# Attention values fetched in token order by five transfers a batch, and seven stage tiles instead of three for the first batch's weights

## The chip, the cores and the metric

The kernel runs on one core of a Trainium2 chip. The metric is the device time of one execution in microseconds (us), lower is better; three executions of the kernel before are at hand, and one further execution was profiled.

## The reference

Three blocks follow one another. Nystrom attention with 32 landmarks over 4 batches of 8 heads, 576 tokens and 64 values a head; then a gated MLP on the 2304 tokens of all batches; then a second MLP.

```python
q_lm = q.reshape(B, H, m, S // m, D).mean(axis=3)      # m = 32, S // m = 18
k_lm = k.reshape(B, H, m, S // m, D).mean(axis=3)
A = sm(q, k_lm); Bm = sm(q_lm, k_lm); C = sm(q_lm, k)  # softmax(scale * a @ b.T)
Z = Bm.T / (norm1(Bm) * norminf(Bm) + 1e-06)
for _ in range(6):
    Z = 2 * Z - Z @ Bm @ Z
x = A @ Z @ C @ v                                      # then to (2304, 512)
xn = x / sqrt(mean(x * x) + 1e-06) * rms_g
x = (silu(xn @ w_gate) * (xn @ w_val)) @ w_out         # d_ff = 1536
out = (s * relu(x @ w_in) ** 2 + b) @ w_out2           # d_ff = 2048
```

The sum over tokens in C @ v may run in any order, if C's columns and v's rows stand in the same one. The weights arrive as 64-bit floats.

## The kernel before

**Order of work.** No engine chooses its work on the chip. While the program is built, a planner (`Scheduler.run`) keeps a list of operations with planned costs, a due key and the buffers that each needs, and writes them one by one into the five engines' queues: the lowest key among those that can start. The queues then run in that order, and an instruction that has to wait holds all that stand behind it in its queue. SyncE (SP) issues nearly all transfers; a transfer's planned cost is split into its landing (all of it) and the hold on SP (the cost less 2.0 us). At most eight transfers are on their way at a time: a ninth is issued when one of the eight has landed.

**Attention.** `attention(b, ...)` is written once for each batch. Batch 0 runs alone at the start; batches 1 to 3 fill gaps of the gated MLP of the batch before. A batch loads k and q by four or more transfers (L458, L463) and v by eighteen (L476): v's tile has tokens on its partitions, and each transfer fills 32 partitions with the 32 tokens of one residue `i * 18 + n`, all heads, as pieces of 256 bytes. C's scores are made in two halves of 288 columns, in that same order of residues; the exponential (L701, ScalarE) writes them side by side into the tile eC, five transposes on TensorE (L718) bring tokens to the partitions, and L740 multiplies with v. v of a later batch goes into the same tile, so its transfers wait for L740 of the batch before.

**The gated MLP.** `units` are pairs of a batch and one of 12 slices f of 128 hidden columns. A unit needs the slice of w_gate and of w_val in single precision, side by side in one of three `rawg` tiles. For batch 0 they come from the 64-bit inputs by `narrow`: a load of 512 KB into a stage tile (L934), three operations of ScalarE on it (L951, L953, L961; the last may go to VectorE as L962), and one of VectorE (L965) that writes the half of rawg. The stage tile is free again after L961. When both halves stand, rawg is stored to DRAM (L978), from where batches 1 to 3 read it (L981); a rawg tile is taken again after its store has landed and after L1034 has read it. L1034 folds the attention's last matrix into the slice (uh, ul through L1044, L1045, L1047), L1059 is the slice's matmuls, L1075, L1077 and L1081 the gating. From unit 6 on, the output matmuls (L1104, L1108) and the narrowing of w_out (L932, tile rawo, store L990, later reads L992) come in between. The second MLP (L1016, L1134) ends the program.

**Stage tiles.** There are three for all uses (`st_r`). The gate and value slices of batch 0 take from a longer ring, in which three more tiles lie in the second half of the buffer xbuf and stay closed until the attention of batch 0 is done:

```python
st_late = [Slot(far[:, :, 256 * i:256 * i + 256].bitcast(I64)) for i in range(3)]
st0_r = Ring(st_r.slots + st_late)
```

The first half of xbuf is written for the first time when the gated MLP's result of batch 0 is evicted (L1118). Up to the planned time 60 the planner also fills gaps of TensorE with matmuls whose result nobody reads (L1291).

Of the kernel before, what the change touches and what calls it, by code (L numbers as in the profile page):

```python
# [37 lines left out]
XC = 2.0  # L38
COLD1 = 6.5
GV = 8  # L40
W2_STEP = 4.2


# [207 lines left out]
def tile_nystrom_attention_two_mlps(  # L251
# [117 lines left out]
    st_late = [Slot(far[:, :, 256 * i:256 * i + 256].bitcast(I64)) for i in range(3)]  # L369
    for x in st_late:  # L370
        x.held = True
    st0_r = Ring(st_r.slots + st_late)

    def xb(c, c0, n):
        return [("x", c, i) for i in range(c0 // 32, (c0 + n) // 32)]
# [34 lines left out]
    def attention(b, t0, t1):  # L410
# [60 lines left out]
            return vs.t.rearrange("p (j h d) -> p j h d", j=5, h=H)  # L471

        def load_v(e):
            sv = v[b].rearrange("h (i n) d -> n i h d", n=SEG)
            for n in range(SEG):
                e.dma_start(out=vt()[32 * (n % 4):32 * (n % 4) + 32, n // 4], in_=sv[token(b, n)])  # L476

        at(("sp", 9.5), -0.25 if b else 0.01, load_v, w=[vs])


        def loaded(g, h):
# [200 lines left out]
        def c_side(g, p0):  # L682
            for j in (g,) if fine else (0, 1) if g == 0 else ():
                transposed("k", j, p0)
            pC = [Buf(ps_r), Buf(ps_r)]
            eC = Buf(eC0_r if first else eC_r)
            cm, cs, rc = Buf(sm_r), Buf(sm_r), Buf(sm_r)
            for hf in range(2):
                scores(pC[hf], "k", g, hf, p0, [(pC[1], "taken")] if hf else [],
                       [(pC[1], "taken"), (eC, "taken")] if hf == 0 else [])  # L690
                at(("dve", t_dve(HC)), p0 + 0.02, lambda e, hf=hf: e.tensor_reduce(
                    out=cm.t[:, hf:hf + 1], in_=pC[hf].t[:, 0:HC], axis=AX, op=ALU.max),
                    r=[pC[hf]], w=[(cm, hf)])

            def c_max(e):
                e.tensor_reduce(out=cm.t[:, 2:3], in_=cm.t[:, 0:2], axis=AX, op=ALU.max)
                e.tensor_scalar(out=cm.t[:, 3:4], in0=cm.t[:, 2:3], scalar1=-scale, scalar2=None, op0=ALU.mult)

            at(("dve", 0.32), p0 + 0.02, c_max, r=[(cm, 0), (cm, 1)], w=[(cm, 3)])
            for hf in range(2):  # L700
                at(("act", t_act(HC) + 0.19), p0 + 0.03, lambda e, hf=hf: e.activation(  # L701
                    out=eC.t[:, HC * hf:HC * hf + HC], in_=pC[hf].t[:, 0:HC], func=ACTF.Exp,
                    scale=scale, bias=cm.t[:, 3:4], accum_out=cs.t[:, hf:hf + 1]),
                    r=[pC[hf], (cm, 3)], w=[(eC, hf), (cs, hf)])

            def c_rec(e):
                e.tensor_tensor(out=rc.t[:, 0:1], in0=cs.t[:, 0:1], in1=cs.t[:, 1:2], op=ALU.add)
                e.tensor_scalar(out=rc.t[:, 0:1], in0=rc.t[:, 0:1], scalar1=1e-9, scalar2=None, op0=ALU.add)
                e.reciprocal(out=rc.t[:, 0:1], in_=rc.t[:, 0:1])

            at(("dve", 0.5), p0 + 0.05, c_rec, r=[(cs, 0), (cs, 1)], w=[rc])
            pE = [Buf(ps_r), Buf(ps_r)]
            eT = Buf(eT_r)

            def tr(_, js):
                for j in js:
                    n = min(128, S - 128 * j)
                    nc.tensor.transpose(  # L718
                        pE[j // 4].t[0:n, 128 * (j % 4):128 * (j % 4) + 128],
                        eC.t[:, 128 * j:128 * j + n], ident)  # L720

            at(("pe", slow * 0.5), p0 + 0.04, lambda e: tr(e, range(4)), r=[(eC, 0), (eC, 1), "ident"],
               w=[pE[0], (pE[1], "taken"), (eT, "taken")])
            at(("pe", 0.13), p0 + 0.04, lambda e: tr(e, [4]), r=[(eC, 1), "ident", (pE[1], "taken")], w=[pE[1]])

            def ev(e, o, i):
                if e is nc.scalar:
                    e.activation(out=o, in_=i, func=ACTF.Copy)
                else:
                    e.tensor_copy(out=o, in_=i)  # L730

            at({"act": t_act(512), "dve": t_dve(512)}, p0 + 0.05, lambda e: ev(e, eT.t[:, 0:512], pE[0].t), r=[pE[0]], w=[(eT, 0)])
            at({"act": t_act(128), "dve": t_dve(128)}, p0 + 0.05, lambda e: ev(e, eT.t[0:64, 512:640], pE[1].t[0:64, 0:128]), r=[pE[1]], w=[(eT, 1)])
            pV = Buf(ps_r)

            def cv_mm(_):
                for j in range(5):
                    n = min(128, S - 128 * j)
                    for h in range(4):
                        nc.tensor.matmul(  # L740
                            out=pV.t[32 * h:32 * h + 32, 0:D],
                            lhsT=eT.t[0:n, 128 * j + 32 * h:128 * j + 32 * h + 32],
                            rhs=vt()[0:n, j, 2 * h + g, :], start=(j == 0), stop=(j == 4))

            at(("pe", 1.3), p0 + 0.06, cv_mm, r=[(eT, 0), (eT, 1), vs], w=[pV, (Cv, "taken")])
            at({"dve": t_dve(64), "act": 0.1 + t_act(64)}, p0 + 0.07, lambda e: (
                e.activation(out=Cv.t[:, D * g:D * g + D], in_=pV.t[:, 0:D], func=ACTF.Copy, scale=rc.t[:, 0:1])
                if e is nc.scalar else e.tensor_scalar(
                    out=Cv.t[:, D * g:D * g + D], in0=pV.t[:, 0:D], scalar1=rc.t[:, 0:1], scalar2=None, op0=ALU.mult)),
                r=[pV, rc], w=[(Cv, g)])  # L750
# [167 lines left out]
    def narrow(key, kind, f, part, dst, w, after=()):  # L918
        c = slice(128 * f, 128 * f + 128)
        wt = ((w_gate, w_val, w_out), (w_in2, None, w_out2))[kind - 1][part]  # L920
        rows = kind == 1 and part < 2
        st, a, m = Buf(st0_r if rows else st_r), Buf(ca_r), Buf(cm_r)

        def wide(x):
            return x.rearrange("p (k f) -> p k f", k=KD) if rows else x

        def staged():
            return wide(st.t) if len(st.t.shape) == 2 else st.t

        def load(e):  # L930
            if part == 2:
                e.dma_start(out=staged(), in_=wt[c, :])  # L932
            else:
                e.dma_start(out=staged() if rows else st.t.rearrange("p (k f) -> p k f", k=KD),  # L934
                            in_=wt[:, c].rearrange("(k p) f -> p k f", p=128))

        def word(i):
            x = staged().bitcast(I32)
            if rows:
                return x.rearrange("p k (n t) -> p k n t", t=2)[:, :, :, i]  # L940
            return x.rearrange("p (n t) -> p n t", t=2)[:, :, i]

        n_ops = len(S_.ops)
        op(("sp", 3.46), key - 12, load, w=[st])
        def low():
            x = staged().bitcast(U8)
            if rows:
                return x.rearrange("p k (n t) -> p k n t", t=8)[:, :, :, 3]
            return x.rearrange("p (n t) -> p n t", t=8)[:, :, 3]

        op(("act", 0.08 + t_act(512)), key, lambda e: e.activation(  # L951
            out=wide(a.t), in_=word(1).bitcast(F32), func=ACTF.Copy, scale=2.0 ** -112), r=[st, "stage"], w=[a])
        op(("act", 0.08 + t_act(512)), key, lambda e: e.activation(  # L953
            out=wide(m.t), in_=low(), func=ACTF.Copy, scale=1.0 / 32, bias=-31.0 / 64), r=[st, "stage"], w=[m])

        def upper():
            return wide(m.t).bitcast(F16).rearrange("p k (n t) -> p k n t", t=2)[:, :, :, 1] if rows else (
                m.t.bitcast(F16).rearrange("p (n t) -> p n t", t=2)[:, :, 1])

        op({"act": 0.08 + t_act(512), "dve": t_dve(512)}, key, lambda e: (  # L960
            e.activation(out=upper(), in_=word(1).bitcast(F32), func=ACTF.Copy, scale=2.0 ** -100)  # L961
            if e is nc.scalar else e.scalar_tensor_tensor(  # L962
                out=wide(m.t), in0=word(1), scalar=-2 ** 31, in1=wide(m.t),
                op0=ALU.bitwise_and, op1=ALU.bitwise_or)), r=[st, m, "stage"], w=[m], pair=True)
        op(("dve", t_dve(512)), key, lambda e: e.scalar_tensor_tensor(  # L965
            out=dst().bitcast(I32), in0=a.t.bitcast(I32), scalar=3, in1=m.t,
            op0=ALU.logical_shift_left, op1=ALU.bitwise_or), r=[a, m, *after], w=[w], pair=True)
        for o in S_.ops[n_ops + 1:]:
            o.after = RELC

# [117 lines left out]
    def out_mm(key, b, hf, f):  # L1088
# [27 lines left out]
        for c in range(KD):  # L1116
            op({"act": t_act(HC), "dve": t_dve(HC)}, key, lambda e, c=c: (
                e.activation(out=xbuf[:, c, c0:c0 + HC], in_=A[c].t[:, 0:HC], func=ACTF.Copy) if e is nc.scalar  # L1118
                else e.tensor_copy(out=xbuf[:, c, c0:c0 + HC], in_=A[c].t[:, 0:HC])),
                r=[A[c], "far"], w=xb(c, c0, HC))  # L1120

    acc = {}

# [103 lines left out]
    for n in range(len(units) + HALF + 1):  # L1227
        t = T[n]
        if n < len(units):
            b, f = units[n]  # L1230
            if f == 0:
                if b + 1 < B:
                    attention(b + 1, *at_time(b + 1))
# [94 lines left out]
```

## Time and profile before

| what | value |
|---|---|
| median of three executions | 877.86 us (877.86 to 879.12) |
| profiled execution, time | 878.94 us |
| profiled execution, span of its instructions | 876.9 us |
| TensorE busy | 850.0 us (97%) |
| VectorE busy | 684.2 us (78%) |
| ScalarE busy | 471.5 us (54%) |
| GpSimd busy | 109.9 us (13%) |
| share of the chain that ended last: TensorE, VectorE, ScalarE, DMA | 82%, 8%, 4%, 2% |
| transferred | 105.96 MB, 121 GB/s over the span |

Busy time is that of instructions of the engine itself; SP only issues and is not counted as busy. The chain that ended last is followed back from the last instruction, at each step to what released it. A busy share over the whole span is a mean over stages with different limits, so the sections below go by stretches of it.

### The profile page before, as it was taken

Reading aid. Unit: us, or ns where it says so; the run is one execution under the profiler, and the core shown is the slowest. Engines: PE = TensorE matmul, PEld = TensorE weight load, DVE = VectorE, ACT = ScalarE, POOL = GpSimd, SP = SyncE. Lnnn points to the kernel's source line nnn. Section 1 sums busy time; section 2 is a strip of 40 time slices with the busy share of each in tenths; the row PEclk is TensorE's granted clock in tenths of the full one; section 3 lists DMA queues with packets and bytes.
Section 4 is the critical chain, followed back from the end, with each engine's and each line's share of the span. In section 5 each row is a group of like instructions: output and inputs, shape, how many; then the busy total and the mean of one; then the engine's idle time right before and its main releaser. Section 6 shows DMA issues by size and latency. Waiting matters only on the chain.

```text
span 876.9 us, 16944 instructions
## 1 busy us (share of the span) xinstructions
PE 850.0 (97%) x6397; PEld 714.7 (82%) x6397; DVE 684.2 (78%) x1494; ACT 471.5 (54%) x968; POOL 109.9 (13%) x148
## 2 busy tenths in 40 slices
PE   8969999999999999999999999999999999999997
PEld 5647767888889888899999888888888888888896
DVE  6868788888998888899999866766676667666786
ACT  4869877346554455478988433433343334333454
POOL 0260046212750123200000000000000000000000
PEclk8989999999999999999999999999999999999999
DMA  7797996876534332369976000010001000100100
GB/s 219 222 350 257 297 272 208 245 232 204 145 112 154 121 99 97 135 202 297 311 229 197 1 1 0 12 37 1 1 15 34 1 1 19 29 1 1 34 16 24
DMA packets 72513, 105.96 MB, mean 121 GB/s; under 512 B 25584, under 2 KB 46064, under 8 KB 72432
## 3 DMA queue, kind: packets, MB, share of 16 engines
q1 hardware_dynamic: 72240, 104.62, 38.4%
q8 instruction: 50, 0.82, 0.4%
q14 instruction: 31, 0.25, 0.1%
q10 hardware_dynamic: 192, 0.26, 0.1%
HBM read 90.70 MB, written 14.16 MB: 120 GB/s over the span
## 4 chain that ended last, share of the span: by engine, by line
PE 82%; DVE 8%; ACT 4%; DMA 2%; issue 2%; SPq 1%; DVEq 0%; ACTq 0%
PE bank L1016 23%; PE bank L1134 22%; PE bank L1059 14%; PE bank L1108 14%; PE bank L1034 3%; PE bank L844 1%; PE bank L1104 1%; PE bank L598 1%; SPq L476 1%; PE bank L660 1%; DMA region<-in_k_dram 1%; PE bank L1291 1%; DVE wl L914 1%; DMA xbuf<-in_moe_w_val_dram 1%; ACT cmag L953 1%
## 5 line engine op out<-in xcount | busy, mean ns | idle before, releaser
L1059 PE MATMUL bank<-xh,uh 128*128 128x288 f32 x384 | 123.1, 320 | 5.6 <-DVE hbuf L1077 4.7
L1269 ACT ACTIVATE hbuf<-bank 128x512 f32<-128x512 f32 (+1 forms) x79 | 43.9, 556 | 144.2 <-PE bank L1016 143.3
L1016 PE MATMUL bank<-xh,uh 128*128 128x512 f32 (+1 forms) x320 | 117.7, 368 | 1.0 <-ACT hbuf L1269 1.0
L1016 PE MATMUL bank<-xh,ul 128*128 128x512 f32 (+1 forms) x320 | 117.7, 368 | 0.0
L1016 PE MATMUL bank<-xl,uh 128*128 128x512 f32 (+1 forms) x320 | 117.6, 368 | 0.0
L1059 PE MATMUL bank<-xl,uh 128*128 128x288 f32 x384 | 113.6, 296 | 0.0
L1059 PE MATMUL bank<-xh,ul 128*128 128x288 f32 x384 | 113.6, 296 | 0.0
L1134 PE MATMUL bank<-wh,hh 128*128 128x512 f32 x288 | 112.4, 390 | 0.3 <-DVE hh L913 0.3
L1134 PE MATMUL bank<-wl,hh 128*128 128x512 f32 x288 | 112.3, 390 | 0.0
L1134 PE MATMUL bank<-wh,hl 128*128 128x512 f32 x288 | 112.0, 389 | 0.0
L1108 PE MATMUL bank<-hh,wh 128*128 128x288 f32 x336 | 101.3, 302 | 0.1
L1108 PE MATMUL bank<-hl,wh 128*128 128x288 f32 x336 | 99.0, 295 | 0.0
L1108 PE MATMUL bank<-hh,wl 128*128 128x288 f32 x336 | 98.8, 294 | 0.2 <-DVE wl L914 0.2
L1059 PEld LDWEIGHTS bank<-xh,uh 128*128 128x128 f32 x384 | 72.7, 189 | 24.9 <-DVE hbuf L1077 6.8
L914 DVE TENSOR_TENSOR hl<-hbuf,hh 128x512 fp32r<-128x512 f32 (+2 forms) x135 | 77.9, 578 | 2.6
L1059 PEld LDWEIGHTS bank<-xl,uh 128*128 128x128 f32 x384 | 72.8, 189 | 0.5
L1059 PEld LDWEIGHTS bank<-xh,ul 128*128 128x128 f32 x384 | 72.6, 189 | 0.0
L1016 PEld LDWEIGHTS bank<-xh,uh 128*128 128x128 f32 x320 | 60.1, 188 | 12.4 <-ACT hbuf L1269 1.2
L1016 PEld LDWEIGHTS bank<-xl,uh 128*128 128x128 f32 x320 | 60.0, 188 | 11.1
L1016 PEld LDWEIGHTS bank<-xh,ul 128*128 128x128 f32 x320 | 60.1, 188 | 10.1
L1108 PEld LDWEIGHTS bank<-hh,wh 128*128 128x128 f32 x336 | 63.0, 188 | 4.4 <-issue 2.3
L913 DVE CAST uh<-region 128x512 fp32r<-128x512 f32 x56 | 23.9, 426 | 54.4 <-PE bank L1016 54.4
(207 smaller groups left out, 1787.6 us busy)
## 6 DMA issues: line engine op xcount, KB each, us to landing
rawo<-kepto SPq DMA_DIRECT2D x84, 256.0 KB, 3.2
rawg<-keptg SPq DMA_DIRECT2D x36, 512.0 KB, 3.9
stage<-in_moe_w_out_dram SPq DMA_DIRECT2D x28, 512.0 KB, 4.6
stage<-in_moe_w_in_dram SPq DMA_DIRECT2D x16, 512.0 KB, 5.0
keptg<-rawg SPq DMA_DIRECT2D x12, 512.0 KB, 6.6
region<-in_v_dram SPq DMA_DIRECT2D x72, 64.0 KB, 2.5
stage<-in_moe_w_val_dram SPq DMA_DIRECT2D x8, 512.0 KB, 6.7
xbuf<-in_moe_w_gate_dram SPq DMA_DIRECT2D x7, 512.0 KB, 7.0
```

The lines of the kernel that those rows point to most:

```text
L476: e.dma_start(out=vt()[32 * (n % 4):32 * (n % 4) + 32, n // 4], in_=sv[token(b, n)])
L598: nc.tensor.matmul(out=ps.t[p, pn * g:pn * g + n], lhsT=lhsT(p, g), rhs=rhs(p, g), start=True, stop=True)
L660: nc.tensor.matmul(out=ps.t[:, 0:HC], lhsT=part(u, "bd")[:, 128 * e:128 * e + 128], rhs=part(y, "t").rearrange("p (t e i) -> p t e i", e=2 ...
L844: nc.tensor.matmul(out=pX2[i].t[:, 0:HC], lhsT=WBD.t[p, 128 * g:128 * g + 128], rhs=AT[hf, g].t[p, 0:HC], start=True, stop=True)
L913: else e.tensor_copy(out=hi(), in_=src())), r=r, w=[wh], pair=True)
L914: b = op({"dve": t_dve(n), "pool": t_pool(n)}, key, lambda e: e.tensor_tensor(out=lo(), in0=src(), in1=hi().bitcast(F32), op=ALU.subtract) ...
L1016: nc.tensor.matmul(out=ps.t[:, 0:n], lhsT=w[a].t[:, ks], rhs=x[y].t[:, kd, 0:n], start=(kd == 0 and i == 0), stop=(kd == KD - 1 and i == 2))
L1034: nc.tensor.matmul(out=pU[g].t[m, 0:256], lhsT=gw[b].t[p, m], rhs=r.t[p, :, 128 * k:128 * k + 128], start=True, stop=True)
L1059: nc.tensor.matmul(out=ps.t[:, 0:HC], lhsT=u[a].t[:, 256 * g + 128 * part:256 * g + 128 * part + 128], rhs=x[y].t.rearrange("p k n -> p (k ...
L1108: nc.tensor.matmul(out=A[c].t[:, 0:HC], lhsT=w[a].t[:, 128 * c:128 * c + 128], rhs=hs[y].t[:, 0:HC], start=(f == 0 and i == 0), stop=(f == ...
L1134: nc.tensor.matmul(out=A[c].t, lhsT=hs[a].t[:, s], rhs=w[y].t, start=(f == 0 and i == 0), stop=(f == F2 - 1 and i == 2))
L1269: e.activation(out=r.t[:, 0:n], in_=ps.t[:, 0:n], func=ACTF.Relu) if e is nc.scalar
```

## The change

v is loaded by five transfers a batch, each of 128 tokens (the last of 64) in the order of the sequence, onto 128 partitions; the pieces of 256 bytes stay. The exponentials of C are written to eC at the columns of their tokens: neighbours in the instruction's order then lie 18 elements apart. The planned cost of v's load falls from 9.5 to 5.0. Four stage tiles in the first half of xbuf are added for batch 0's gate and value slices, open from the start. A gate in the planner's list, at the first unit of batch 1, keeps evictions that are listed after it behind all operations on these tiles.

```diff
+V_SP = 5.0
-    st0_r = Ring(st_r.slots + st_late)
+    st_near = [Slot(xbuf[:, :, 256 * i:256 * i + 256].bitcast(I64)) for i in range(4)]
+    st0_r = Ring(st_r.slots + st_near + st_late)
+    row_ops = []
         def load_v(e):
-            sv = v[b].rearrange("h (i n) d -> n i h d", n=SEG)
-            for n in range(SEG):
-                e.dma_start(out=vt()[32 * (n % 4):32 * (n % 4) + 32, n // 4], in_=sv[token(b, n)])
-        at(("sp", 9.5), -0.25 if b else 0.01, load_v, w=[vs])
+            for j in range(5):
+                n = min(128, S - 128 * j)
+                e.dma_start(out=vt()[0:n, j], in_=v[b][:, 128 * j:128 * j + n].rearrange("h n d -> n h d"))
+        at(("sp", V_SP), -0.25 if b else 0.01, load_v, w=[vs])
+            def in_order(hf):
+                x = eC.t[:, 0:S]
+                if fine:
+                    return x.rearrange("p (i n) -> p n i", i=M)[:, HB * hf:HB * hf + HB]
+                return x.rearrange("p (i t e) -> p e t i", i=M, e=2)[:, hf]
-                    out=eC.t[:, HC * hf:HC * hf + HC], in_=pC[hf].t[:, 0:HC], func=ACTF.Exp,
+                    out=in_order(hf), in_=pC[hf].t[:, 0:HC].rearrange("p (t i) -> p t i", i=M), func=ACTF.Exp,
+        if rows:
+            row_ops.extend(S_.ops[n_ops:])
-                r=[A[c], "far"], w=xb(c, c0, HC))
+                r=[A[c], "far", "near"], w=xb(c, c0, HC))
+            if n == F1:
+                gate("near", row_ops, t)
```

## Rows read from the trace of the kernel before

**Rows 1.** Busy time of each engine by stretch, granted clock, DMA share.

```profile
10.00:20.00 10.00, 7.79 (x123) 4.15 (x122) 7.96 (x33) 4.15 (x13) 0.67 (x1) 0.84 0.60 150
...
42.26:80.00 37.74, 28.99 (x262) 23.23 (x261) 27.69 (x62) 28.35 (x60) 14.76 (x21) 0.91 0.89 300
...
80.00:130.00 50.00, 48.34 (x577) 33.98 (x575) 40.13 (x110) 41.78 (x94) 10.50 (x14) 1.00 0.93 281
130.00:240.00 110.00, 106.90 (x1041) 90.75 (x1041) 96.80 (x224) 60.33 (x136) 44.72 (x57) 1.00 0.69 212
```

**Rows 2.** Timeline of SP's issues, 0 to 60 us: start, duration, line, transfer, count.

```profile
2.67 13.33 SPq L476 DMA_DIRECT2D region<-in_v_dram  x18
16.05 0.45 SPq L934 DMA_DIRECT2D stage<-in_moe_w_gate_dram  x1
...
18.23 0.79 SPq L395 DMA_DIRECT2D gT<-in_moe_rms_g_dram  x1
...
28.92 14.54 SPq L476 DMA_DIRECT2D region<-in_v_dram  x18
43.55 0.40 SPq L934 DMA_DIRECT2D stage<-in_moe_w_val_dram  x1
...
47.09 1.66 SPq L978 DMA_DIRECT2D keptg<-rawg  x1
```

**Rows 3.** The chain that ended last, 36 to 82 us: start, duration, what.

```profile
43.55 4.91 DMA stage<-in_moe_w_val_dram
...
57.01 2.88 PE bank L1059 x12
...
61.38 1.78 PE bank L1059 x12
```

**Rows 4.** Timeline of ScalarE, with the idle time before and what ended it.

```profile
17.44 0.50 ACT L701 ACTIVATE region<-bank,region 128x288 f32<-128x288 f32 x1 [1.46 <-DVE region L697]
...
20.50 0.66 ACT L951 ACTIVATE ca<-stage 128x512 f32<-128x512 f32 x1 [1.98 <-DMA stage<-in_moe_w_gate_dram]
...
48.48 0.67 ACT L951 ACTIVATE ca<-stage 128x512 f32<-128x512 f32 x1 [3.14 <-DMA stage<-in_moe_w_val_dram]
```

**Rows 5.** Timeline of TensorE.

```profile
25.03 1.31 PE L740 MATMUL bank<-region 128*32 128x64 f32 x40
...
42.26 0.51 PE L1059 MATMUL bank<-xh,uh 128*128 128x288 f32 x1
...
53.18 1.22 PE L1034 MATMUL bank<-rawg,gw 64*32 64x256 f32 x16 [3.31 <-DVE hbuf L1077]
```

**Rows 6.** Matmuls of L1291 alone, by stretch: busy time of TensorE first.

```profile
42.26:80.00 37.74, 2.73 (x11) 1.41 (x11) 0.91 0.89 300
```

**Rows 7.** Transfers from 11 to 16 us, when only v's eighteen moved: packets, share of 16 engines.

```profile
DMA packets 2241, 0.56 MB, mean 111 GB/s; under 512 B 2240, under 2 KB 2240, under 8 KB 2240
...
q1 hardware_dynamic: 2240, 0.54, 48.4%
```

**Rows 8.** Groups of ScalarE's instructions, 42.26 to 80 us: count, busy us, mean ns.

```profile
L961 ACT ACTIVATE cmag<-stage 128x512 f16<-128x512 f32 x7 | 5.5, 782 | 0.1
```

**Rows 9.** Groups of VectorE's instructions, 42.26 to 80 us.

```profile
L965 DVE SCALAR_TENSOR_TENSOR rawg<-ca,cmag 128x512 int32<-128x512 int32 x11 | 9.3, 849 | 3.3 <-ACT cmag L961 3.3
```

**Rows 10.** Stores of line L978, 43.5 to 70 us: from issue to landing.

```profile
DMA to landing us min/median/max: 5.3/8.7/9.5
```

**Rows 11.** Timeline of VectorE.

```profile
56.04 1.89 DVE L965 SCALAR_TENSOR_TENSOR rawg<-ca,cmag 128x512 int32<-128x512 int32 x2
```

**Rows 12.** The chain that ended last, 146 to 164 us.

```profile
146.96 0.42 SPq L476
...
156.11 0.45 SPq L476
...
156.67 3.17 DMA rawo<-kepto
```

**Rows 13.** Timeline of TensorE, 144 to 166 us: the rows with idle time before them.

```profile
156.81 0.40 PE L1059 MATMUL bank<-xh,uh 128*128 128x288 f32 x1 [1.31 <-DVE hbuf L1077]
```

## The prediction

> **What bounds the kernel now.** I read the page's 40 slices first, then busy time by stretch, then the chain that ended last, then the queue of SP, then single engines where the chain pointed. The page says TensorE, 97% of the span; by stretch that is true from 80 us on, and untrue before. From 42.26 us, where the first matmul of the gated MLP starts [rows 5], to 80 us TensorE is busy for 28.99 of 37.74 us, while the DMA engines are at 0.89 [rows 1]. Of the busy time 2.73 us are filling matmuls [rows 6], and twelve matmuls of L1059 took 2.88 us at 57 us where twelve took 1.78 us at 61 us [rows 3]; the granted clock, 0.91 over the stretch [rows 1], had fallen to the lower of its two levels after the long gap. So some 8.75 + 2.73 + 1.1 = 12.6 us of this stretch are no work. After it TensorE idles 1.66 of 50 us and 3.1 of 110 us.
>
> Why it idles is read from the chain: at 43.55 us a load of a value slice is issued and waited for during 4.91 us [rows 3]. ScalarE stands 3.14 us for it [rows 4], and TensorE 3.31 us before L1034 of the third slice [rows 5]. The load was not late because the memory was slow: SP issued v of batch 1 from 28.92 to 43.46 us, eighteen transfers, and the load stood behind them [rows 2]. Batch 0's v had held SP from 2.67 to 16.00 us in the same way. While only v moved, the DMA engines were 48% busy [rows 7]: idle bandwidth, then a queue at full share.
>
> **The change part by part.**
>
> *v's issue.* Before, 18 instructions hold SP for 13.33 us and 14.54 us (batches 0 and 1) [rows 2], and for some 9.6 us in batch 2, 146.96 to 156.56 us [rows 12]. After, 5. What is unknown is the price of an issue with 1024 pieces. Lower end: an issue of a stage load, 512 pieces, takes 0.45 us [rows 2], as one of v's 256 pieces does in row 156.11 [rows 12]; with some 0.04 us between issues five take 2.5 us. Upper end: gT's issue, 512 pieces of 4 bytes, took 0.79 us [rows 2]; if the price grew with the pieces, 0.45 us for 256 would be 1.8 us for 1024, and five would hold SP for 9 us, little less than now. I take the lower end, since the larger stage load pays no more, but not less than the moving itself where free places among the eight run out: 2240 pieces in 5 us at 48.4% of 16 engines are 17.3 ns each [rows 7], so the 576 x 8 = 4608 pieces of a batch need 5.0 us of all engines. SP is held for 2.5 to 5 us, and what stands behind batch 1's v is issued some 10 us earlier.
>
> A rule bears on this: the Trainium skill, "DMA: Bandwidth & Descriptors", section "Issuing engines are not separate DMA queues", calls the time to initiate a DMA usually small beside the DMA itself. By it this part would be worth nothing; batch 2's rows, 9.6 us of issue for 5.0 us of moving, say that it is not small here.
>
> *Four stage tiles.* With three, slice 2's value part could be loaded only at 43.55 us. With seven, the first seven loads follow v directly: 512 KB at the 300 GB/s of the busy stretch [rows 1] are 1.7 us, so seven need 12 us, and v at 5 us more than k and q would be in at about 15 us; all seven have landed by about 28 us, where before the value part of slice 2 came at 48.46 us (43.55 + 4.91 [rows 3]). The engines' bytes stay the same; they move into idle share between 10 and 45 us (0.60 in 10 to 20 us [rows 1]).
>
> *What is late next.* Not the loads, then, but what follows them: a rawg tile is free only after its store. The store of slice 0 is issued at 47.09 us behind the loads [rows 2], stores land in 5.3 to 9.5 us [rows 10], and L965 of slice 3 follows at 56.04 us [rows 11]. With SP free at about 34 us that store leaves some 10 us earlier, too. After that VectorE and ScalarE set the pace: 27.69 and 28.35 us of work in the 37.74 us [rows 1]. One to two parts of narrowing can move ahead of 42 us: for ScalarE at most 2 x (0.67 + 0.67 + 0.78) = 4.2 us of busy time (the middle operation taken as like the first [rows 4, 8]), for VectorE 0.85 to 1.7 us [rows 9]. VectorE, then, keeps about 26.5 us. In 130 to 240 us it runs at 96.80 / 110 = 88% beside a full TensorE [rows 1]; at that share 26.5 us take 30 us. Gain: 37.7 - 30 = 7.7 us; I take 7.5. Ends: 3.3 us if only the hole before L1034 closes [rows 5], 11 us if VectorE ran without gaps (37.7 - 26.5).
>
> *v of batches 2 and 3.* Batch 2's eighteen issues lie on the chain, and a load of w_out's kept copy stands behind them [rows 12]; TensorE loses 1.31 us there [rows 13]. I take 1.2 us of it, the ends being nothing and all. For batch 3 I found no idle TensorE behind v, and take nothing.
>
> *Exponentials in token order.* 16 instructions of 0.50 us [rows 4] now write with a stride of 72 bytes. No row has such a stride. Ends: nothing, or twice the time, 0.5 us each. Batch 0 has four; L740, the user of the first pair, starts at 25.03 us [rows 5], 7 us after the first exponential, with VectorE's chain in between, so I take nothing, at most +1 us. Later ones lie in an engine with 60.33 of 110 us used [rows 1], and cost nothing. The first transposes of a pair must wait for both halves: up to 0.5 us, in the same cover. v itself is no gain to L740: it was there long before.
>
> The Trainium skill, "SBUF - State Buffer", section "Door 1: The DMA port swizzle", says that each access to a new line of 16 bytes pays a penalty, which a stride of 72 bytes does every time. No run here shows it yet; by the doubled price above the sum would lose that 1 us at most.
>
> *Narrowing inside attention 0.* Loads that land early put their operations into ScalarE's queue between those of the attention, as the first one did at 20.50 us, with 1.98 us of waiting before it [rows 4]. ScalarE has 5.85 us to spare between 10 and 20 us [rows 1]; operations of 0.7 us that come just ahead of an exponential delay it by half of that. Ends: -0.8 us (fewer of them after 34 us, where they stand in front of the last square roots) to +3 us (below). I take +0.5 us.
>
> *Given back.* From 80 to 130 us DMA is at 0.93 and ScalarE at 41.78 of 50 us [rows 1]. Units that come earlier find the same bytes to move. I take +0.7 us, ends 0 and +4.
>
> The gate and the ring cost no instruction. Sum: -7.5 - 1.2 + 0.5 + 0.7 = -7.5 us. The profiled execution took 878.94 us (span 876.9 and 2.0 around it), 1.1 us over the median; against it 871.4 us, against the median of 877.86 us **870.4 us**.
>
> **The rivals.** The measurement tells about 0.2%, 1.8 us, from no change.
>
> 1. *Only the hole closes.* The store of rawg, in SP's order behind loads that now run ahead, stays the limit: slices 3 to 5 still wait for it. For it: stores landed in 8.7 us (median) [rows 10]. Against it: that was with the engines full. Or an issue of 1024 pieces costs 1.8 us. Gain 3.3 us less what is given back: 1.8 to 4.5 us, 873.4 to 876 us.
>
> 2. *DMA-bound anyway.* The bytes are the same, and at 0.93 to 130 us the time until batch 1's slices come from the kept copies can't shrink. For it the 0.93; against it: 0.60 in 10 to 20 us, 4 us of all engines unused in ten, and TensorE at 48.34 of 50 us where DMA stood at 0.93 [rows 1]. Gain given back, 876 to 879 us.
>
> 3. *Slower: a stall of ScalarE in attention 0.* The planner holds that a load lands 3.46 us after issue; the first stage load took until 20.50 us, 4.4 us after its issue at 16.05 us [rows 2, 4], and the one of 43.55 us 4.91 us [rows 3]. With v also planned as landed after 5 us, a narrowing operation can stand in ScalarE's queue, unlanded, in front of the softmax that VectorE's chain waits for. Each slice part so placed costs about 2 us, as the wait of 1.98 us [rows 4]; from four such on (8 us) the gain is gone and the result is slower. Time: 880 to 884 us. Against it: VectorE's own chain, 7.96 of 10 us busy in 10 to 20 us [rows 1], gives a load time to land.
>
> 4. *More.* VectorE without gaps, and the shortened front carries on: gain over 12 us, below 866 us.
>
> **How the numbers follow.** The forecast (gain of 4.5 to 12 us, 866 to 873.4 us): 0.55. Rival 1: 0.20, rival 2: 0.08, rival 3: 0.12, rival 4: 0.05. The forecast's own range is 866 to 873.4 us. The range that leaves out rival 3, the upper half of rival 2 and most of rival 4 is 865 to 878 us. Faster by over 0.2%: 0.55 + 0.20 + 0.05 = 0.80; within: 0.08; slower: 0.12.
>
> **What would show it.** SP's timeline: v in five issues of about 0.45 us, batch 1's done before 35 us; seven stage loads before 28.92 us. ScalarE: no wait of 3 us for a value slice after 42 us. TensorE: L1034 of the third slice before 49 us instead of 53.18 us, the clock at its upper level from 50 to 60 us, the sixth L1034 some 8 us earlier. The first L1059 at 42.26 us, give or take 1 us; if it comes later than 45 us, rival 3 is at work. From 80 us on the same order of work, shifted. The prediction is wrong if issues of v take over 1.5 us, if L965 of slice 3 still comes after 53 us, or if the stretch from 80 to 130 us grows by what the one before lost.

## The result and the profile after

The changed kernel takes 889.16 us (median; 886.4 to 889.25) where the kernel before took 878.0 us beside it: a ratio of 1.0123, 95% interval 1.0107 to 1.014. The forecast was 870.4 us, a gain. The span of the profiled execution grew from 876.9 to 887.5 us.

Busy time by stretch, of the kernel after; the columns are those of [rows 1]:

```profile
10.00:20.00 10.00, 6.90 (x124) 4.52 (x123) 7.41 (x32) 7.28 (x19) 0.67 (x1) 0.99 1.20 268
20.00:30.00 10.00, 6.46 (x71) 3.23 (x71) 2.09 (x9) 4.21 (x10) 0.00 (x0) 0.50 0.71 222
30.00:40.00 10.00, 7.61 (x163) 5.26 (x167) 7.76 (x30) 3.99 (x9) 4.02 (x6) 0.50 0.78 299
...
42.26:80.00 37.74, 32.24 (x298) 25.08 (x296) 29.98 (x67) 33.85 (x73) 15.43 (x21) 0.95 0.94 282
80.00:130.00 50.00, 44.78 (x542) 31.69 (x541) 36.63 (x98) 43.73 (x92) 4.37 (x5) 0.97 0.86 271
130.00:240.00 110.00, 106.29 (x1041) 89.47 (x1039) 96.47 (x231) 60.70 (x136) 42.38 (x57) 1.00 0.69 199
```

The front carries more bytes, as meant (268 GB/s in 10 to 20 us; 150 before [rows 1]). But VectorE works only 2.09 of the 10 us after 20 us, and TensorE's granted clock is at the lower of its levels for 20 us. The second loss lies in 80 to 130 us, where TensorE is busy for 3.6 us less than before [rows 1].

VectorE's timeline says what it stood for (idle time and its end in brackets):

```profile
22.88 0.15 DVE L706 TENSOR_SCALAR region<-region 128x1 f32<-128x1 f32 x1
25.29 0.48 DVE L780 STREAM_TRANSPOSE xbuf<-bank 128x288 f32<-128x288 f32 x1 [2.26 <-DMA xbuf<-in_moe_w_val_dram]
25.70 0.25 DVE L646 SCALAR_TENSOR_TENSOR region<-region,bank 128x128 f32<-128x128 f32 x1
31.10 0.45 DVE L781 TENSOR_REDUCE region<-xbuf 128x9 f32<-128x288 f32 x1 [5.16 <-DMA xbuf<-in_moe_w_gate_dram]
...
96.72 0.46 DVE L1092 SCALAR_TENSOR_TENSOR xbuf<-hbuf,bank 128x288 f32<-128x288 f32 x1 [3.39 <-DMA xbuf<-in_moe_w_val_dram]
```

L780 and L781 are the softmax of attention 0. They write and read its transposed scores in the far half of xbuf; the loads fill near tiles. They share no byte, and yet the one waits for the other. On the chain that ended last the two loads, 13.22 us together, are the largest pieces between 15 and 56 us:

```profile
17.20 8.01 DMA xbuf<-in_moe_w_val_dram
25.25 0.05 issue
25.29 0.48 DVE xbuf L780
25.80 5.21 DMA xbuf<-in_moe_w_gate_dram
31.10 0.13 DVE region L781
```

SP's timeline answers to [rows 2]:

```profile
2.68 8.44 SPq L479 DMA_DIRECT2D region<-in_v_dram  x5
...
15.65 0.38 SPq L943 DMA_DIRECT2D xbuf<-in_moe_w_val_dram  x1
...
17.20 2.95 SPq L943 DMA_DIRECT2D xbuf<-in_moe_w_val_dram  x1
25.80 0.37 SPq L943 DMA_DIRECT2D xbuf<-in_moe_w_gate_dram  x1
...
28.39 1.93 SPq L461 DMA_DIRECT2D region<-in_q_dram  x2
43.64 0.33 SPq L989 DMA_DIRECT2D keptg<-rawg  x1
44.06 5.00 SPq L479 DMA_DIRECT2D region<-in_v_dram  x5
```

The wait ran both ways. The load at 25.80 us had itself waited 5.7 us, by the waits of SP, for VectorE's L646 at 25.70 us, which stood behind the first stall. From 30.3 to 43.6 us SP stands before a store of rawg, late because VectorE is late. Both stand among the waits of SP, 0 to 60 us (total, times, longest):

```profile
SPq L989 <- DVE rawg L974: 13.2, 1, 13.2
SPq L943 <- DVE region L646: 5.7, 1, 5.7
```

v of batch 1, due behind that store, goes out 15 us later than before (44.06 for 28.92 us). About half of that comes from the false wait, the one between instructions that share no byte: in the run with row tiles, below, v stands behind the same store and goes out at 36.62 us.

The groups of v's issues (ns min/median/max) and of ScalarE's exponentials (count, busy us, mean ns):

```profile
L479 SPq DMA_DIRECT2D region<-in_v_dram x20: 384/1046/4221, 2.7 to 231.2; - x20
```

```profile
L710 ACT ACTIVATE region<-bank,region 128x288 f32<-128x288 f32 x14 | 10.0, 796 | 0.0
```

An issue of v costs 1.05 us in the median, not 0.45, and the shortest, with 1024 pieces, 0.38 us. An exponential takes 796 ns; the same group of the kernel before:

```profile
L701 ACT ACTIVATE region<-bank,region 128x288 f32<-128x288 f32 x14 | 6.8, 493 | 1.5 <-DVE region L697 1.5
```

### The profile page after: what moved, and what is told of

Its sections match the earlier page's. It is cut to its first block, busy times and chain, and to the rows that moved or that the text cites. A ratio compares the mean times of both kernels' runs of the same rounds, so it can differ in the third digit from the quotient of the medians.

```text
span 887.5 us, 16900 instructions
## 1 busy us (share of the span) xinstructions
PE 854.2 (96%) x6395; PEld 717.2 (81%) x6395; DVE 683.7 (77%) x1491; ACT 478.8 (54%) x973; POOL 109.6 (12%) x148
## 4 chain that ended last, share of the span: by engine, by line
PE 77%; DVE 9%; ACT 6%; DMA 3%; issue 2%; SPq 2%; POOL 0%; DVEq 0%; ACTq 0%
PE bank L1145 22%; PE bank L1027 21%; PE bank L1070 13%; PE bank L1119 12%; PE bank L1045 2%; DMA xbuf<-in_moe_w_val_dram 1%; ACT ca L960 1%; PE bank L663 1%; ACT cmag L962 1%; PE bank L601 1%; PE bank L853 1%; SPq L479 1%; PE bank L1115 1%; DVE wl L923 1%; ACT cmag L970 1%
## 5 line engine op out<-in xcount | busy, mean ns | idle before, releaser
L1070 PE MATMUL bank<-xh,uh 128*128 128x288 f32 x384 | 123.0, 320 | 3.5 <-DVE hbuf L1088 1.6
L1070 PE MATMUL bank<-xl,uh 128*128 128x288 f32 x384 | 113.7, 296 | 0.0
L1070 PE MATMUL bank<-xh,ul 128*128 128x288 f32 x384 | 113.5, 296 | 0.0
L1070 PEld LDWEIGHTS bank<-xh,uh 128*128 128x128 f32 x384 | 72.8, 190 | 23.6 <-DVE wh L922 3.7
L1070 PEld LDWEIGHTS bank<-xl,uh 128*128 128x128 f32 x384 | 72.8, 190 | 0.5
L1070 PEld LDWEIGHTS bank<-xh,ul 128*128 128x128 f32 x384 | 72.6, 189 | 0.0
```

The lines of the kernel that those rows point to most:

```text
L1070: nc.tensor.matmul(out=ps.t[:, 0:HC], lhsT=u[a].t[:, 256 * g + 128 * part:256 * g + 128 * part + 128], rhs=x[y].t.rearrange("p k n -> p (k ...
```

## The experiments

Each ratio is to the kernel before on the same chip, with its 95% interval.

**Whole rows in place of pieces.** A near tile of the change is four pieces, 256 columns in each row of xbuf; here it is one run of 1024 columns in one row. The tiles cover the same bytes together, and on every engine the instructions stand in the same order as in the changed kernel.

```
-    st_near = [Slot(xbuf[:, :, 256 * i:256 * i + 256].bitcast(I64)) for i in range(4)]
+    st_near = [Slot(xbuf[:, i, 0:1024].bitcast(I64)) for i in range(4)]
```

> The changed kernel with one line edited: each of the four added stage tiles is one run of 1024 columns in one row of xbuf, instead of 256 columns in each of the four rows. The five queues hold the same instructions in the same order; only the addresses and the waits differ. Theory 1 (waits between tiles that share no byte: a load into a tile of four pieces, and the attention's tiles that lie in xbuf between those pieces, are held to overlap): VectorE's waits of 2.3 and 5.2 us for loads into xbuf are gone, the first matmul of the gated MLP starts some 8 us earlier, and the time is 872 to 881 us. Theory 2 (the order of the queues is worse: loads and narrowing stand in front of the attention's work): the same waits at the same places, 886 to 890 us.

878.88 us, 1.0003 (0.999 to 1.0015): 10.3 us come back by the shape of four tiles alone. VectorE's rows in this run:

```profile
22.49 0.29 DVE L646 SCALAR_TENSOR_TENSOR region<-region,bank 128x128 f32<-128x128 f32 x1 [2.12 <-ACT cmag L970]
22.70 0.15 DVE L705 TENSOR_REDUCE region<-region 128x1 f32<-128x2 f32 x1
22.88 0.15 DVE L706 TENSOR_SCALAR region<-region 128x1 f32<-128x1 f32 x1
22.95 0.47 DVE L780 STREAM_TRANSPOSE xbuf<-bank 128x288 f32<-128x288 f32 x1
...
24.18 0.45 DVE L781 TENSOR_REDUCE region<-xbuf 128x9 f32<-128x288 f32 x1
```

The rows from L646 to L706 agree with those of the changed kernel to 0.01 us; then L780 follows at once, and L781 6.9 us earlier than after. The load itself is no faster: that of 17.20 us took 8.0 us from issue to landing in the changed kernel and 7.9 us here. The first gated matmul starts at 44.14 us instead of 51.71, 7.6 us; the wait before L1092 late in batch 0 shrinks from 3.39 to 0.6 us, 2.8 us. Together that is 10.4 us of the 11.8 us between the spans of the two profiled executions (887.5 and 875.7 us). What remains is no gain.

**The two parts apart.** First the v loads and exponentials without the near tiles, then the near tiles without the v part, once in pieces as in the change and once as rows.

```
 e2:  st0_r = Ring(st_r.slots + st_late)              # v and exponentials of the change
 e3:  st0_r = Ring(st_r.slots + st_near + st_late)    # v and exponentials of before
 e4:  as e3, st_near = [... xbuf[:, i, 0:1024] ...]
```

> The kernel before with the v part of the change alone (five transfers, exponentials in token order, planned cost 5.0), and no added stage tiles. Theory 1: no wait of VectorE for a load into xbuf before the gated MLP starts; SP is free of batch 1's v some 8 us earlier; 873 to 878 us. Theory 3 (the v part costs the time: exponentials of 0.80 us instead of 0.49 us in front of the attention's chain, and issues of v that hold SP while eight transfers are on their way): 880 to 889 us.

> The kernel before with the added stage tiles alone, in four pieces as in the change; v is loaded by eighteen transfers and the exponentials are written as before. Theory 1: VectorE waits for loads into xbuf in the attention of batch 0, 882 to 890 us. Theory 3: no slower than before, 873 to 879 us.

> As the kernel with the added stage tiles alone, but each tile is one run of 1024 columns in one row of xbuf; the queues hold the same instructions in the same order as there. Theory 1: 5 to 12 us faster than that kernel, 872 to 879 us. Theory 2: within 1 us of it.

The v part: 878.33 us, 1.0 (0.9988 to 1.0013). Tiles in pieces: 895.34 us, 1.0196 (1.0175 to 1.0216). Row tiles: 878.96 us, 1.0003 (0.9984 to 1.0022). The whole loss is the tiles' and goes with their shape, 16.4 us here. The longest waits of VectorE with pieces, 0 to 60 us (total, times, longest):

```profile
DVE xbuf L773 <- DMA xbuf<-in_moe_w_val_dram: 4.8, 1, 4.8
DVE region L779 <- DMA xbuf<-in_moe_w_gate_dram: 3.8, 1, 3.8
```

Neither is in the run with rows. Theory 1 had the sign of the tiles' loss and not its size: 882 to 890 us, and 5 to 12 us back with rows.

The v part's nothing is a sum of losses and gains. Its first slice starts at 40.8 us instead of 37.8, but its sixth at 71.6 us instead of 75.6. That lead is lost by the ninth slice, 105.6 us instead of 101.0. In between VectorE waits twice before L1091, which writes hidden values into xbuf (L1092 of the changed kernel), the second time for a load into a late tile, which is in pieces too:

```profile
85.45 0.45 DVE L1091 SCALAR_TENSOR_TENSOR xbuf<-hbuf,bank 128x288 f32<-128x288 f32 x1 [2.54 <-DMA kepto<-rawo]
...
97.86 0.46 DVE L1091 SCALAR_TENSOR_TENSOR xbuf<-hbuf,bank 128x288 f32<-128x288 f32 x1 [2.88 <-DMA xbuf<-in_moe_w_gate_dram]
```

Batch 1, from its first slice to batch 2's, then takes 110.0 us instead of 112.1 (starts of each slice's first matmul, L1045 of the changed kernel).

**Narrowing later in the order.** With row tiles the loads were early and the narrowing was not: VectorE did its operation of the first two parts at 34.88 us and of the third at 39.10 us (33.00 and 37.22 us before). The planner's release of the narrowing was put 20 us later, to take it out of attention 0, in the whole change and in the tiles alone.

```
-RELC = 0
+RELC = 20.0
```

> The kernel with row tiles (v part and added tiles as one run each), with one number edited: the planner may start no narrowing operation before its time 20 (RELC, before 0). Where the 12 us of TensorE's loss went after the false waits are gone: theory A (two parts narrowed between 16 and 22 us stand in ScalarE's queue in front of the exponentials and push the end of batch 0's attention back by 2 us): the first matmul of the gated MLP comes at 42 to 43 us instead of 44.1, and the time is 1 to 3 us lower, 875.5 to 878 us. Theory B (the two ca and two cmag tiles keep loaded slices from being narrowed ahead, so ScalarE is full from 45 to 75 us whatever was loaded): no change or slower by up to 2 us, since the two parts narrowed early are now narrowed later.

> The added tiles alone, one run each, v by eighteen transfers and exponentials of 0.49 us, and no narrowing before the planner's time 20. Theory A: 1 to 3 us lower than the same kernel with narrowing from 0, 876 to 878 us. Beside the kernel with late narrowing and the v part it shows what the v part brings once the tiles are there: by the 1.31 us that TensorE lost behind batch 2's v in the kernel before, 0 to 1.5 us.

879.55 us, 1.0011 (0.9996 to 1.0026), and 879.33 us, 1.0014 (1.0 to 1.0028): no gain, though the first of them starts its first slice at 34.6 us and its eighth at 85.6 us (39.7 and 88.4 us with the narrowing in its place, 37.8 and 89.7 us before the change). The row of VectorE where it loses the lead:

```profile
90.30 0.45 DVE L1092 SCALAR_TENSOR_TENSOR xbuf<-hbuf,bank 128x288 f32<-128x288 f32 x1 [5.28 <-DMA xbuf<-in_moe_w_gate_dram]
```

L1092 writes hidden values into a tile at the end of a row; the load fills a late tile, and those are still in pieces. It is the same wait in another place, and the kernel before has it as well (waits of VectorE, 60 to 160 us):

```profile
DVE xbuf L1081 <- DMA xbuf<-in_moe_w_val_dram: 1.6, 1, 1.6
```

**A third pair of narrowing tiles.** Three near row tiles, and the fourth row for another ca and cmag, with the narrowing in its old place and 20 us later.

```
+    ca0_r = Ring(ca_r.slots + [Slot(xbuf[:, 3, 0:512])], True)
+    cm0_r = Ring(cm_r.slots + [Slot(xbuf[:, 3, 512:1024].bitcast(I32))], True)
```

> The kernel with row tiles, with three ca and three cmag tiles for the gate and value slices of batch 0 instead of two; the third pair lies in the row of xbuf that was the fourth added stage tile, so six stage tiles are open at the start. Theory B: five or six parts are narrowed before 42 us instead of four, ScalarE is less full from 45 to 75 us, and the time is 2 to 5 us lower, 874 to 877 us. Theory A: the parts stand in front of the attention as before, the first matmul of the gated MLP stays at 44 us or comes later, 878 to 881 us.

> Three ca and three cmag tiles, and no narrowing before the planner's time 20. If both theories hold, 872 to 876 us; if only A, as the kernel with the late narrowing alone, within 1 us.

893.84 us, 1.0186 (1.0162 to 1.021), and 886.4 us, 1.0097 (1.0078 to 1.0117). As a test of the pairs these runs failed: the new tiles lie inside the span of the late tiles' pieces, and in the first of them ScalarE waited 6.8 us for a load of xbuf before an operation on the third pair. They show the false wait once more, and nothing about pairs.

**No tile in pieces.** Row tiles, and the late tiles left out of the ring; with the narrowing in its place, with it 20 us later, with three pairs, and without the v part.

```
-    st0_r = Ring(st_r.slots + st_near + st_late)
+    st0_r = Ring(st_r.slots + st_near)
```

> The stage tiles of batch 0 as whole row pieces (as in the run with row tiles) and the three late tiles, which are still four pieces each, left out of the ring. Theory 1 (waits between tiles that share no byte are the whole loss, and the late tiles still cost some): no wait of VectorE on xbuf is ended by a stage load any more, and the time is 874 to 878 us. Theory 2 (ScalarE's queue sets the pace of batch 0 from the first gated matmul on, and the late tiles are only where the wait shows): 878 to 880 us, as with the late tiles. Rival: the late tiles carried loads ahead, and without them it is slower, over 881 us.

> The same, with the narrowing put 20 us later in the planner's order. With the late tiles this order had its slices 11 us ahead in the middle of batch 0 and lost it at a write of hidden tiles that waited 5.3 us for a late tile's load. Theory 1: without late tiles the gain is kept in part, 868 to 875 us. Theory 2: VectorE and ScalarE take it back anyway at the end of batch 0's first half, 877 to 881 us.

> Three near row tiles, and a third pair of tiles for the narrowing in the fourth row, with no late tiles: no tile of it is in pieces. Theory A (the two pairs of narrowing tiles hold the parts that are narrowed before attention 0 ends to two): a third part is narrowed before 34 us and the time is 3 to 6 us under that of the run without late tiles, 869 to 874 us. Theory B (VectorE is full until 34 us whatever tiles there are): two parts before 34 us, and within 1.5 us of that run.

> Row tiles alone, v and exponentials as before the change, no late tiles, narrowing 20 us later. Theory 1: 869 to 876 us, at or below the run with the whole change in this form, since its sixteen exponentials take 0.50 and not 0.80 us. If v's order is worth its 5 us of the front, it is 2 to 4 us above that run instead. Theory 2: 877 to 880 us.

| run | us | ratio | interval |
|---|---|---|---|
| no late tiles | 875.44 | 0.9973 | 0.9963 to 0.9984 |
| and narrowing later | 874.5 | 0.9959 | 0.9946 to 0.9972 |
| and three pairs | 874.48 | 0.9962 | 0.995 to 0.9974 |
| no v part, narrowing later | 875.31 | 0.9969 | 0.9956 to 0.9982 |

All four beat both kernels, by 2.8 to 3.8 us against 878.28. Busy time of the first:

```profile
42.26:80.00 37.74, 31.84 (x320) 24.89 (x320) 31.54 (x83) 35.54 (x75) 15.89 (x21) 1.00 0.93 290
80.00:130.00 50.00, 47.65 (x548) 33.50 (x548) 39.91 (x100) 43.45 (x92) 11.19 (x15) 1.00 0.93 288
130.00:240.00 110.00, 108.66 (x1067) 93.38 (x1067) 94.66 (x222) 62.06 (x137) 42.00 (x51) 1.00 0.65 191
```

No wait of VectorE for a load of xbuf is left, which theory 1 said. But ScalarE is busy for 35.54 of 37.74 us (28.35 before [rows 1]), so theory 2's pace-setter is there as well. Moving the narrowing changed 0.9 us, less than the intervals tell apart. In the run with three pairs the third part is narrowed inside attention 0, as theory A said (ScalarE, then VectorE):

```profile
22.35 0.63 ACT L962 ACTIVATE xbuf<-stage 128x512 f32<-128x512 f32 x1
...
26.56 0.76 ACT L972 ACTIVATE xbuf<-stage 128x512 f16<-128x512 f32 x1
```

```profile
34.99 1.28 DVE L976 SCALAR_TENSOR_TENSOR rawg<-ca,cmag 128x512 int32<-128x512 int32 x2
36.19 0.68 DVE L976 SCALAR_TENSOR_TENSOR rawg<-xbuf 128x512 int32<-128x512 int32 x1
```

The operation of VectorE still comes at 36 us, when attention 0 lets go of it, and the time is within 1 us: theory B's number; a gain of 3 to 6 us is refuted.

**Late tiles left out without near ones.** These two ask where the 3 us come from.

```
 e13: -    st0_r = Ring(st_r.slots + st_late)     # kernel before
      +    st0_r = Ring(st_r.slots)
 e14: the same, with v and exponentials of the change
```

> The kernel before with its three late tiles left out of the ring, nothing else changed. Theory A (the four near tiles are worth some 3 us once no tile of the ring is in pieces): this run has no near tiles, so it stays at 877 to 879 us or is slower, since loads wait for the four remaining tiles. Theory B (all of the 3 us is the waits that the late tiles cause, in the kernel before too): 874 to 876 us. Rival: the late tiles are worth more than their waits cost, 881 us or more.

> The v part alone (loads and exponentials), with the three late tiles left out of the ring. If v's order is worth nothing by itself, within 1.5 us of the kernel before without its late tiles. If the earlier end of the v loads at the front is worth something once stage loads can't run ahead into late tiles, 2 us or more under that run.

893.38 us, 1.0165 (1.0148 to 1.0182), and 889.09 us, 1.0117 (1.0097 to 1.0137). Without any extra tile the kernel before loses 14.3 us, by the rival's reason: from 80 to 130 us TensorE is busy for 43.05 us (48.34 [rows 1]), and DMA is at 0.80.

```profile
80.00:130.00 50.00, 43.05 (x500) 30.75 (x501) 36.85 (x94) 31.25 (x71) 14.46 (x20) 0.97 0.80 231
```

So the 3 us aren't got by dropping the late tiles as such: with row tiles in their place their loads run ahead as well. That the late tiles' waits are the 3 us is not shown: beside row tiles VectorE had only 0.6 us of such waits left, and of the 3.0 us between the spans of the two profiled executions (875.7 and 872.7 us) 1.6 us arise in batch 1, which takes 111.2 us with the late tiles and 109.6 us without. The v part is worth 4.3 us here, where loads can't run ahead; beside row tiles I can't tell it from nothing (874.5 and 875.31 us).

## Why the prediction was wrong

**The step that failed** is "The gate and the ring cost no instruction." No working instruction was added, true; waits were, and I costed none. I took tiles without a common byte for independent. A tile in pieces was treated as lying across everything between its first and its last piece: I infer that from where the waits fell, and the runs show the effect (10.3 us by the shape alone), not the rule by which the program gets its waits. The kernel before already showed such a wait, 1.6 us before L1081, among the waits of VectorE from 60 to 160 us. I read chain and timeline up to 82 us and not that list, where a write into xbuf waits for a load into another tile of it.

**The size of the gain** was wrong too, even without the waits. In the run with row tiles, waits gone at the front, TensorE works 32.41 of the 37.74 us, 3.53 of it filling, so 28.88 us against 28.99 - 2.73 = 26.26 us [rows 1, 6]: 2.6 us, not 7.5.

```profile
42.26:80.00 37.74, 32.41 (x315) 25.77 (x313) 30.07 (x76) 34.35 (x73) 15.41 (x21) 0.95 0.97 311
```

Rival 1's 3.3 us were the better number. I let VectorE set the pace, since both engines had some 28 us of work; here ScalarE has 34.35 and VectorE 30.07. My "one to two parts of narrowing can move ahead" did not happen: two parts were ahead of the first gated matmul's slice already, and a third, in the run with three pairs, brought 1.0 us, less than the intervals tell apart.

**Narrowing inside attention 0 and the exponentials.** I had +0.5 and nothing; row tiles alone start the first slice 1.9 us later than before, the v part alone 3.0 us, both together 1.9 us. One piece is visible: 2.12 us of VectorE before L646, ended by L970, a narrowing operation of ScalarE, rival 3's mechanism at a quarter of its price. The exponentials' doubled price, my upper end, was the nearer one: +0.30 us each, +0.03 us for the read of the sum behind each, 1.3 us for batch 0's four. With the rule that I cited from the Trainium skill, "SBUF - State Buffer", section "Door 1: The DMA port swizzle", the trace agrees in direction; it shows 0.30 us for 288 columns at a stride of 72 bytes.

**v's issue.** I took 0.45 us; the first batch's five come near the upper end of 9 us (8.44 us), the median of one is 1.05 us. But the reason that I gave for that end, a price that grows with the pieces, isn't the one: the first issue of each of the four batches, with 1024 pieces too, took 0.38 to 0.53 us. What makes the later ones longer is not shown. Two of my bounds were crossed for that (an issue over 1.5 us, batch 1's done before 35 us); the second was crossed by the store in front, not by the issue. The rule of the Trainium skill, "DMA: Bandwidth & Descriptors", section "Issuing engines are not separate DMA queues", that the time to initiate a DMA is usually small beside the DMA, fits the short ones; the median of 1.05 us and the longest of 4.22 us, against 5.3 us in the median from issue to landing, do not agree.

**v of batch 2** came out near in number, by luck as far as is known: the whole change shortens batch 1 by 1.1 us (112.1 to 111.0); I had 1.2, for TensorE's idle time of 1.31 us [rows 13]. Most of that idle time is still there:

```profile
169.50 0.40 PE L1070 MATMUL bank<-xh,uh 128*128 128x288 f32 x1 [0.96 <-DVE hbuf L1088]
```

In the v part alone it is gone, and batch 1 is 2.1 us shorter. But batch 1 is shorter also in two runs that load v as before: 110.0 us without late tiles, 110.4 us with row tiles, no late tiles and narrowing later. So its length does not show what v is worth there.

**Right in part:** the hole before the third slice closed with row tiles, as the part on the four tiles said, but TensorE's wait for VectorE behind the second slice's L1045 grew to 2.54 us (1.57 before), and the third slice starts at 55.0 us, not before 49. **Given back** was sized at 0.7 us and is the other term that was too small: with row tiles the sixth slice is 3.6 us early (72.0 for 75.6 us) and batch 1's first 0.2 us (148.7 for 148.9), so nearly all of it went. Leaving out the late tiles got 3.4 us (878.88 to 875.44 us).

**The rivals.** My sign to watch, the first L1059 later than 45 us, came true (51.71 us; L1070 now), but rival 3 named the wrong engine: VectorE stood, not ScalarE, and for another cause, and 889 us lies above its 884. No rival held the mechanism. Open stay why the first slice starts later in all three runs, since such a wait stands in the two with the v part (1.93 us in the v part alone) and not in that with row tiles alone, and whether ScalarE is what now limits batch 0: no run was made that takes work off it.

## What to carry to other kernels

Before buffers are packed into the gaps of another buffer, list every wait between instructions on that buffer and ask whether they share a byte: an extra buffer is free only if nothing else waits for it. Prefer tiles that are one run in memory, and test one that isn't by giving it that shape with the order of instructions kept. An earlier load brings only as much as the next engine in line can take up, and two engines at equal busy time mean that either may set the pace.

## What the runs showed of the hardware

An exponential of 128x288 that writes with a stride of 72 bytes took 796 ns where the contiguous write took 493 ns, and its sum's read 232 ns against 200 ns. The twenty issues of v, sixteen of them with 1024 pieces, held their queue for 0.38 to 4.22 us, median 1.05 us, the first of each batch for 0.38 to 0.53 us; the transfers landed 3.4 to 8.4 us after issue.
